# The second exchange of a spectral layer, read back by quarters of the partitions

## The chip, the cores and the metric

The kernel runs on one core of a Trainium2 chip. A core has five engines that run side by side, each through its own list of instructions in order: PE (matrix multiply), DVE and ACT (elementwise work), POOL (more elementwise work) and SP (here it only issues transfers). They share a memory of 128 partitions (SBUF); PE writes into a separate accumulator memory (PSUM) from which DVE and ACT copy. Transfers (DMA) to and from the chip's main memory (DRAM) are issued by SP or ACT and run on 16 transfer engines. An engine waits for another, or for a transfer, at a semaphore. The metric is the device time of one execution in microseconds (us); lower is better.

## The reference

Four layers on a sequence of 2048 rows of 512 values: spectral, attention, spectral, attention, each added to its input.

```python
def _A_ref(x, w_r, w_i):
    B, S, D = x.shape
    X = rfft2(x)                       # over rows and columns
    X = X * (w_r + 1j * w_i)
    return irfft2(X, s=(S, D))
...
x = A_x
x = x + _A_ref(_layernorm(x), A_w_r, A_w_i)
x = x + _B_ref(_layernorm(x), B_wq, B_wk, B_wv, B_wo)
x = x + _A_ref(_layernorm(x), A_w_r, A_w_i)
x = x + _B_ref(_layernorm(x), B_wq, B_wk, B_wv, B_wo)
```

`_A_ref` is the spectral layer, `_B_ref` an attention of 32 heads with one shared key and value. S is 2048 and D is 512.

## The kernel before

Row n of the sequence is 16 p + t: partition p (0 to 127) of tile t (0 to 15). The spectral layer does both transforms as matrix multiplies. The 256 frequencies over the columns are worked on in two halves, h = 0 and 1, of 128 frequencies, real and imaginary part side by side (256 values). The transform over the 2048 rows is split as 128 x 16: `first` sums over p within each tile; then partitions and tiles must change places (the first exchange, through the DRAM tensor D1, with `cross1`); `filtered(j)` sums over the 16 tiles and multiplies by the weights; `back(j)` begins the inverse, 16 points wide; then partitions and tiles change places again (the second exchange, through D2); `along(q, h)` sums over the 128 remaining points with the table CS, two tiles at a time; `last` transforms the columns back and adds x.

The second exchange is what the change is about. Step j of `filtered` and `back` stands for half h = j // 4 and for four of sixteen values of b, 4 (j % 4) to 4 (j % 4) + 3. `back(j)` makes two banks of two b each on PE (lines 213 to 215), ACT copies them to the tile B1 (line 365; DVE does the very last, line 363), and SP writes each copy to D2 (line 366), 128 KB a time; so a half has eight writes. In B1 a partition is (t, a), a from 0 to 7. For `along` the partition must be m = 16 a + b and the tile t. `cross2(h, g)` (line 369) reads tiles 4g to 4g + 3 of half h for all 128 partitions into B2, 256 KB in runs of 512 bytes. Its source spans every b, so each of the four readings depends on all eight writes of its half.

The order of the work is written out by hand: a spectral layer runs under a manual schedule for PE, ACT, DVE and SP, so each engine's instructions stand in the order of the program text. The string STEPS gives the order of `filtered` (f), `back` (b), `joined` (j, the last products of a filter step) and the readings of half 0 (x):

```python
STEPS = "f0 f1 f2 b0 f3 b1 b2 j3 b3 x0 f4 f5 f6 b4 f7 b5 j7 b6 b7"
```

Behind it PE does `along` for half 0, tiles 0 to 15 (line 391, copied to the tile AT by ACT, line 394, and DVE, line 396, in turn). Then come the four readings of half 1: g = 0 and 2 issued by SP, g = 1 and 3 by ACT, behind ACT's four copies. SP goes on with the attention's weights wq and wo (lines 1215 and 1216, in the first spectral layer only). PE does `last` for half 0 of tiles 0 to 3 (lines 404 to 406), then `along` for half 1, one pair of tiles at a time with `last` for both halves of the pair before. The sum goes to x (ACT, line 425), DVE takes the statistics for the next layer norm (line 156), and the keys, values and queries of the attention follow.

In `along`, the contraction is over the 128 partitions of B2, that is over m, against the rows of CS:

```python
nc.tensor.matmul(ps[:, i, :], lhsT=B2[:, h, 2 * q + i, 128 * j:128 * j + 128], rhs=CS[:, j, :], ...
```

The framework tracks which bytes each transfer and instruction reads and writes and puts in the waits; the engine that issues a transfer waits for what the transfer depends on, and everything behind it in that engine's list waits too.

Of the kernel before, what the change touches and what calls it, by code (L numbers as in the profile page):

```python
# [11 lines left out]
P = 128  # L12
BF = mybir.dt.bfloat16
# [32 lines left out]
VCELLS = 128  # L46
LASTW = 6
NEGATE = 7
STEPS = "f0 f1 f2 b0 f3 b1 b2 j3 b3 x0 f4 f5 f6 b4 f7 b5 j7 b6 b7"
NORMED, NORMG = (1,), ((3,), (3,), (3,))  # L50
OUTK, LATE_AT = 2, 4
TWICE = ((7,), 8)
# [23 lines left out]
def host_tables():  # L76
    import ml_dtypes
    bf = lambda a: np.ascontiguousarray(np.asarray(a, dtype=np.float32).astype(ml_dtypes.bfloat16))
    tabs = {}
    p = np.arange(P, dtype=np.float64)  # L80
    m = np.arange(P, dtype=np.float64)
    t16 = np.arange(16, dtype=np.float64)

    row = (128 * np.arange(4)[None, :, None] + np.arange(P)[:, None, None]).astype(np.float64)
    ff = (np.arange(256)[None, None, :] + 1).astype(np.float64)

    half = 2 * np.pi * np.arange(256) / 512.0
    cos, sin = np.cos(half), np.sin(half)
    cos[128], sin[0] = 0.0, 0.0
    cos[129:], sin[129:] = -cos[1:128][::-1], sin[1:128][::-1]  # L90
    turn = (row * ff).astype(np.int64) % 512
    c, s = np.concatenate([cos, -cos])[turn], -np.concatenate([sin, -sin])[turn]
    tabs["PH"] = bf(np.concatenate([c[..., :128], s[..., :128], c[..., 128:], s[..., 128:]], axis=2))

    ang = 2 * np.pi * (16 * p[:, None, None] + t16[None, :, None]) * m[None, None, :] / 2048.0
    tabs["C1"], tabs["S1"] = bf(np.cos(ang)), bf(np.sin(ang))

    ti, ai = np.divmod(np.arange(P), 8)
    same = (ai[:, None] == ai[None, :]).astype(np.float64)
    ang = 2 * np.pi * ti[:, None] * ti[None, :] / 16.0  # L100
    tabs["G"] = bf(np.stack([same * np.cos(ang), same * np.sin(ang), -same * np.sin(ang)], axis=1))

    b16 = np.arange(16, dtype=np.float64)
    mm = 16 * ai[:, None, None] + b16[None, :, None]
    ang = 2 * np.pi * (ti[:, None, None] * t16[None, None, :] / 16.0 + t16[None, None, :] * mm / 2048.0)
    tabs["HC"] = bf(np.stack([np.cos(ang), np.sin(ang), -np.sin(ang)], axis=1))
    tabs["mask8"] = bf(ai[:, None] == np.arange(8)[None, :])

    ang = 2 * np.pi * m[:, None] * p[None, :] / 128.0
    tabs["CS"] = bf(np.stack([np.concatenate([np.cos(ang), np.sin(ang)], axis=1),  # L110
                              np.concatenate([-np.sin(ang), np.cos(ang)], axis=1)], axis=1))

    frow = (128 * np.arange(2)[None, :, None] + np.arange(P)[:, None, None] + 1).astype(np.float64)
    dd = np.arange(512)[None, None, :].astype(np.float64)
    ang = 2 * np.pi * frow * dd / 512.0
    cf = np.where(frow == 256, 1.0, 2.0) / (S * D)
    tabs["PSC"] = bf(cf * np.cos(ang))
    tabs["PSS"] = bf(-cf * np.sin(ang))
    tabs["ident"] = bf(np.eye(P, dtype=np.float32))
    tabs["hmask"] = (np.arange(P)[:, None] // DH % 2 == np.arange(2)[None, :]).astype(np.float32)  # L120
    return tabs


class Tables:


    def __init__(self, nc):
        self.nc, self.host, self.dram = nc, host_tables(), {}
# [82 lines left out]
def rotate(nc, ps, c, s, sn, re_im, first):  # L211

    nc.tensor.matmul(ps, lhsT=c, rhs=re_im, start=True, stop=False, skip_group_check=True)  # L213
    nc.tensor.matmul(ps[:, 0:128], lhsT=s, rhs=re_im[:, 128:256], start=False, stop=False, skip_group_check=True)
    nc.tensor.matmul(ps[:, 128:256], lhsT=sn, rhs=re_im[:, 0:128], start=False, stop=True, skip_group_check=True)  # L215


def spectral_layer(nc, tc, tabs, ht, A_w_r, A_w_i, x_sb, bigp, pre, norm, att, feed, weights):
    C1, S1, S1N, PH, ident = (tabs[n] for n in ("C1", "S1", "S1N", "PH", "ident"))
    with tc.tile_pool(name="workA", bufs=2) as work, tc.tile_pool(name="tabA", bufs=1) as tabA, \  # L220
# [30 lines left out]
            weights(k)  # L251

        D1 = dram.tile([2, 16, P, 256], BF, name="D1")
        D2 = dram.tile([2, P, 16, 256], BF, name="D2")
        turned = len(feed.xT)
        xT = feed.xT[0] if turned else bigp.tile([P, NC, 16, P], BF, name="xT", tag="big")
        Pk, A1, A2 = big("Pk"), big("A1"), big("A2")
# [67 lines left out]
        Z, B1, B2 = big("Z"), big("B1"), big("B2")  # L325
        M = big("M").rearrange("p h t c -> p (h t c)").rearrange("p (i j b r f) -> p i j b r f", i=2, j=4, b=4, r=2)

        def filtered(j):

            h, b4 = j // 4, 4 * (j % 4)  # L330
            hf = slice(128 * h, 128 * h + 128)
            X = work.tile([P, 4, 2, 128], BF, name="X", tag="X", bufs=3)
            for b in range(b4, b4 + 4, 2):
                ps = bank()
                for i in range(2):
                    rotate(nc, ps[:, i, :], G[:, 0, :], G[:, 1, :], G[:, 2, :], A2[:, h, b + i, :], i == 0)
                nc.scalar.copy(out=X[:, b - b4:b - b4 + 2, :, :], in_=ps.rearrange("p j (r f) -> p j r f", r=2))
            m1, m2 = (M[:, i, j % 4] for i in range(2))
            wrb = wr_sb[:, b4:b4 + 4, hf].unsqueeze(2).to_broadcast([P, 4, 2, 128])
            wib = wi_sb[:, b4:b4 + 4, hf].unsqueeze(2).to_broadcast([P, 4, 2, 128])  # L340
            nc.vector.tensor_tensor(out=m1, in0=X, in1=wrb, op=ALU.mult)
            joined()
            nc.vector.tensor_tensor(out=m2, in0=X, in1=wib, op=ALU.mult)
            products.append((j, m1, m2))
# [3 lines left out]
        def joined():  # L348

            while products:  # L350
                j, m1, m2 = products.pop()
                Zv = Z[:, j // 4, 4 * (j % 4):4 * (j % 4) + 4, :].rearrange("p b (r f) -> p b r f", r=2)
                nc.vector.tensor_tensor(out=Zv[:, :, 0, :], in0=m1[:, :, 0, :], in1=m2[:, :, 1, :], op=ALU.subtract)
                nc.vector.tensor_tensor(out=Zv[:, :, 1, :], in0=m1[:, :, 1, :], in1=m2[:, :, 0, :], op=ALU.add)  # L354

        def back(j):
            h, b4 = j // 4, 4 * (j % 4)
            for b in range(b4, b4 + 4, 2):
                ps = bank()
                for i in range(2):  # L360
                    rotate(nc, ps[:, i, :], H1[:, b + i, :], H2N[:, b + i, :], H2[:, b + i, :], Z[:, h, b + i, :], i == 0)
                if j == 7 and b > b4:
                    nc.vector.tensor_copy(out=B1[:, h, b:b + 2, :], in_=ps)
                else:
                    nc.scalar.copy(out=B1[:, h, b:b + 2, :], in_=ps)
                nc.sync.dma_start(out=D2[h, :, b:b + 2, :], in_=B1[:, h, b:b + 2, :])

        def cross2(h, g, eng):
            eng.dma_start(out=B2[:, h, 4 * g:4 * g + 4, :],
                          in_=D2[h].rearrange("(t a) b c -> t (a b) c", t=16)[4 * g:4 * g + 4].rearrange("t m c -> m t c"))  # L370

        for step in STEPS.split():
            j = int(step[1])
            if step[0] == "f":
                filtered(j)
            elif step[0] == "b":
                back(j)
            elif step[0] == "j":
                joined()
            else:  # L380
                for g in range(4):
                    cross2(0, g, nc.sync)

        AT = big("AT").rearrange("p h t c -> p (h t c)").rearrange("p (t h c) -> p t h c", t=16, h=2)

        def along(q, h, use_scalar):

            ps = bank()
            for i in range(2):
                for j in range(2):  # L390
                    nc.tensor.matmul(ps[:, i, :], lhsT=B2[:, h, 2 * q + i, 128 * j:128 * j + 128], rhs=CS[:, j, :],  # L391
                                     start=(j == 0), stop=(j == 1), skip_group_check=True)
            if use_scalar:
                nc.scalar.copy(out=AT[:, 2 * q:2 * q + 2, h, :], in_=ps)
            else:
                nc.vector.tensor_copy(out=AT[:, 2 * q:2 * q + 2, h, :], in_=ps)
# [10 lines left out]

        for q in range(8):
            along(q, 0, q % 2 == 0)
        for g in range(4):  # L410
            cross2(1, g, (nc.sync, nc.scalar)[g % 2])
        weights(20)
        early = 4
        for t in range(early):
# [2 lines left out]
        for q in range(9):  # L417
# [9 lines left out]
            g, odd = divmod(q - 3, 2)  # L427
# [746 lines left out]
def full_kernel(ctx, tc, A_x, A_w_r, A_w_i, B_x, B_wq, B_wk, B_wv, B_wo, out):  # L1174
# [63 lines left out]
    for layer in range(2):  # L1238
        norm_in, norm_out = make_norm(), make_norm()
        spectral_layer(nc, tc, tabs, ht, A_w_r, A_w_i, x_sb, bigp, norm, norm_in, att, feed,  # L1240
                       weights if layer == 0 else lambda k: None)
        feed = attention_layer(nc, tc, att, norm_in, norm_out, x_sb, wo_sb, None if layer == 0 else store)
        norm = norm_out
# [47 lines left out]
```

## Time and profile before

| | us |
|---|---|
| median of 3 runs | 1403.82 (1402.8 to 1404.65) |
| the profiled execution, its time | 1403.77 |
| the profiled execution, its span | 1402.0 |
| PE busy | 1352.2 (96%) |
| ACT busy | 1331.0 (95%) |
| DVE busy | 1309.9 (93%) |
| POOL busy | 844.2 (60%) |

The span runs from the first instruction to the last; the time of an execution has something around it. Busy times are sums over the whole span, most of which is attention. The two spectral layers take roughly the first 90 us and the stretch from about 700 to 785 us. In these the engines are less full, and the transfer engines carry most of what they move in the whole program: 32.62 MB in all.

In lines of the timeline the first two numbers are the start and the duration; then come engine, line, operation, output and inputs, and the number of instructions merged. "SPq" and "ACTq" are the issuing of transfers by SP and ACT, "PEld" the loading of weights into PE. In square brackets stands how long the engine was idle before, and what ended that. "To landing" is the time from the issue of a transfer to its completion.

### The profile page before, as it was taken

Reading aid. Unit: us, or ns where it says so; the run is one execution under the profiler, and the core shown is the slowest. Engines: PE = TensorE matmul, PEld = TensorE weight load, DVE = VectorE, ACT = ScalarE, POOL = GpSimd, SP = SyncE. Lnnn points to the kernel's source line nnn. Section 1 sums busy time; section 2 is a strip of 40 time slices with the busy share of each in tenths; the row PEclk is TensorE's granted clock in tenths of the full one; section 3 lists DMA queues with packets and bytes.
Section 4 is the critical chain, followed back from the end, with each engine's and each line's share of the span. In section 5 each row is a group of like instructions: output and inputs, shape, how many; then the busy total and the mean of one; then the engine's idle time right before and its main releaser. Section 6 shows DMA issues by size and latency. Waiting matters only on the chain.

```text
span 1402.0 us, 34913 instructions
## 1 busy us (share of the span) xinstructions
PE 1352.2 (96%) x14118; PEld 471.5 (34%) x14118; DVE 1309.9 (93%) x2269; ACT 1331.0 (95%) x1542; POOL 844.2 (60%) x503
## 2 busy tenths in 40 slices
PE   7899999999999999999998999999999999999998
PEld 6652232222222222222276422232222222222222
DVE  5689999999999999999966899999999999999997
ACT  6679999999999999999966899999999999999997
POOL 3225666667666667666640267666667667666664
PEclk9999999999999999999999999999999999999999
DMA  8700000000000000001064000000000000000000
GB/s 237 205 24 2 1 2 2 2 1 2 2 2 1 2 2 2 1 1 37 12 173 129 1 2 2 2 2 9 5 6 2 6 9 5 1 5 6 9 2 16
DMA packets 45394, 32.62 MB, mean 23 GB/s; under 512 B 10160, under 2 KB 43312, under 8 KB 44720
## 3 DMA queue, kind: packets, MB, share of 16 engines
q1 hardware_dynamic: 42832, 29.18, 7.3%
q8 instruction: 110, 1.80, 0.5%
q10 hardware_dynamic: 2400, 1.21, 0.3%
q14 instruction: 52, 0.43, 0.1%
HBM read 18.32 MB, written 10.49 MB: 21 GB/s over the span
## 4 chain that ended last, share of the span: by engine, by line
ACT 46%; PE 38%; issue 8%; DVE 6%; DMA 1%; POOL 0%; SPq 0%; DVEq 0%; ACTq 0%
ACT e L1089 45%; PE pv L878 14%; PE sc L923 12%; DVE ph L963 2%; PE aux L923 2%; PE ps L273 2%; PE aux L462 1%; DVE ln_stats L156 1%; PE ps L213 1%; PE aux L691 1%; PE pv L893 1%; DMA B<-D 1%; DVE ph L995 1%; PE ps L391 1%; DMA x_sb<-in_A_x_dram 1%
## 5 line engine op out<-in xcount | busy, mean ns | idle before, releaser
L1089 ACT ACTIVATE e<-sc 128x1024 bf16<-128x1024 f32 x1328 | 1218.1, 1164 | 2.9 <-PE sc L923 2.9
L987 POOL TENSOR_TENSOR ph<-ph,step 128x1024 int32<-128x1024 int32 x404 | 762.8, 1891 | 413.0 <-DVE ph L995 295.8
L963 DVE TENSOR_SCALAR ph<-aux 128x512 uint16<-128x512 f32 x1440 | 905.8, 682 | 20.4 <-PE aux L923 16.2
L878 PE MATMUL pv<-ph,vaug 128*32 128x512 bf16 x4320 | 548.7, 386 | 0.7 <-POOL ph L987 0.3
L923 PE MATMUL sc<-QT,Kv 32*128 32x512 bf16 x2656 | 522.0, 380 | 19.4 <-ACT e L1089 13.9
L878 PE MATMUL pv<-e,vaug 128*32 128x512 bf16 x2656 | 484.0, 384 | 0.3 <-ACT e L1089 0.3
L923 PE MATMUL aux<-QT,Kv 32*128 32x512 bf16 x1440 | 455.9, 384 | 0.0
L923 PEld LDWEIGHTS <-Kv 32*128 32x128 bf16 x4096 | 183.2, 91 | 526.0 <-issue 517.7
L893 PE MATMUL pv<-wo_sb,zeros 128*32 128x512 bf16 x1200 | 257.8, 383 | 0.0
L878 PEld LDWEIGHTS <-vaug 128*32 128x32 bf16 x6976 | 147.6, 94 | 292.6 <-issue 281.6
L995 DVE TENSOR_SCALAR ph<-ph 128x2048 uint16<-128x2048 uint16 x316 | 217.6, 689 | 0.5
L162 POOL TENSOR_TENSOR ln_rstd<-ln_veps,mhalf 128x4 f32<-128x4 f32 x16 | 16.5, 1032 | 109.8 <-DVE ln_veps L161 109.7
L156 DVE BATCH_NORM_STATS2 ln_stats<-x_sb 128x6 f32<-128x512 bf16 x64 | 43.5, 680 | 20.1 <-ACT x_sb L425 14.0
L893 PEld LDWEIGHTS <-zeros 128*32 128x32 bf16 x1200 | 60.1, 94 | 1.9 <-issue 0.3
L793 DVE STREAM_TRANSPOSE oT<-pv 128x512 f32<-128x512 f32 x64 | 45.6, 713 | 9.2 <-PE pv L878 9.2
L185 ACT ACTIVATE Pk<-ps,ln_rstd 128x256 bf16<-128x256 f32 x64 | 26.8, 473 | 19.7 <-PE ps L273 15.2
L462 PE MATMUL aux<-xTa,wq_sb 128*128 128x512 bf16 x120 | 39.5, 385 | 0.4 <-DVE ph L963 0.2
L273 PE MATMUL ps<-tab_PH,xT 128*128 128x256 bf16 x256 | 35.3, 286 | 1.1 <-DVE oT L793 0.8
L287 DVE CAST A<-ps 128x512 bf16<-128x512 f32 x28 | 19.2, 689 | 18.2 <-PE ps L215 17.1
L691 PE MATMUL aux<-wo_sb,ph 128*128 128x512 bf16 x96 | 31.8, 384 | 1.5 <-DVE ph L963 1.0
L815 POOL TENSOR_TENSOR on<-oT,rden 128x512 bf16<-128x512 f32 x30 | 31.7, 1056 | 2.0 <-DVE rden L819 1.8
L213 PE MATMUL ps<-Z,tab_H 128*128 128x256 bf16 x64 | 15.8, 283 | 13.2 <-DVE Z L354 13.2
(109 smaller groups left out, 697.7 us busy)
## 6 DMA issues: line engine op xcount, KB each, us to landing
D<-A SPq DMA_DIRECT2D x32, 128.0 KB, 2.7
A<-D SPq DMA_DIRECT2D x16, 256.0 KB, 3.4
D<-B SPq DMA_DIRECT2D x32, 128.0 KB, 2.9
B<-D SPq DMA_DIRECT2D x12, 256.0 KB, 3.7
wr_sb<-in_A_w_r_dram SPq DMA_DIRECT2D x2, 1024.0 KB, 6.1
wi_sb<-in_A_w_i_dram SPq DMA_DIRECT2D x2, 1024.0 KB, 8.2
out_dram<-x_sb SPq DMA_DIRECT2D x15, 128.0 KB, 1.7
x_sb<-in_A_x_dram SPq DMA_DIRECT2D x3, 512.0 KB, 8.2
```

Of the source, the lines that this page charges most:

```text
L156: nc.vector.bn_stats(st, src)
L273: nc.tensor.matmul(ps[:, j, :], lhsT=xT[:, cc, 2 * k + j, :], rhs=PH[:, cc, 256 * h:256 * h + 256], start=(cc == 0), stop=(cc == NC - 1), ...
L462: self.nc.tensor.matmul(ps, lhsT=w(c), rhs=self.xTq[:, c, qc * 512:(qc + 1) * 512], start=(c == 0), stop=(c == NC - 1), skip_group_check=True)
L691: nc.tensor.matmul(ps, lhsT=OTs[qb][:, g4, kk * P:(kk + 1) * P], rhs=wo_sb[:, g4, :], start=first, stop=last, skip_group_check=True)
L793: end = clock.now(clock.FLIP, lambda: nc.vector.transpose(out=oT[:, par].rearrange("p b c -> p (b c)"), in_=pv), clock.last + clock.MM_END)
L878: nc.tensor.matmul(pv_tiles[gi][32 * i:32 * i + 32, :], lhsT=vaug[:, kc, j, :], rhs=es, start=((gi, i) not in started), stop=(left[gi, i] ...
L893: nc.tensor.matmul(pv_tiles[gi][32 * i:32 * i + 32, :], lhsT=att.zeros, rhs=wo_sb[:, 0, :], start=False, stop=False, skip_group_check=True)
L923: nc.tensor.matmul(out, lhsT=Kv[r, par, kc * P:(kc + 1) * P], rhs=QT[r, g, qb * 512:(qb + 1) * 512], start=True, stop=True, skip_group_che ...
L963: end = clock.now(clock.Z, lambda: nc.vector.tensor_scalar(out=z.bitcast(U16), in0=ps, scalar1=SCALE * LOG2E * 128.0, scalar2=127.0 * 128. ...
L987: nc.gpsimd.tensor_tensor(out=copy.bitcast(I32), in0=z.bitcast(I32), in1=step.to_broadcast([P, w // 2]), op=ALU.add)
L995: nc.vector.tensor_scalar(out=one.bitcast(U16), in0=z.bitcast(U16), scalar1=float(PHASE[1]), scalar2=None, op0=ALU.add)
L1089: nc.scalar.activation(out=e[:, 0:ng * 512], in_=sc[:, 0:ng, :].rearrange("p a b -> p (a b)"), func=ACT.Exp, scale=SCALE)
```

## The change

The readings of the second exchange become quarters of the partitions in place of quarters of the tiles. Quarter g of half h holds the four b that step j = 4 h + g wrote, for all a, and all 16 tiles; so it depends on two writes. D2 gets the shape [2, 4, 128, 4, 256], a block for each step; a write still moves 1 KB for each partition. A reading still moves 256 KB in runs of 512 bytes, now into 32 partitions with 16 tiles each. Partition 32 g + 4 a + b' of B2 then holds m = 16 a + 4 g + b', and the rows of the table CS, made on the host, are put in the same order.

The eight readings are steps of STEPS, all issued by SP: x0 to x3 (half 0) stand together behind b3, where the four readings stood; x4 stands behind b6, and x5, x6 and x7 behind b7. None is left behind `along` of half 0, and none on ACT.

```diff
-STEPS = "f0 f1 f2 b0 f3 b1 b2 j3 b3 x0 f4 f5 f6 b4 f7 b5 j7 b6 b7"
+STEPS = "f0 f1 f2 b0 f3 b1 b2 j3 b3 x0 x1 x2 x3 f4 f5 f6 b4 f7 b5 j7 b6 x4 b7 x5 x6 x7"
...
-                              np.concatenate([-np.sin(ang), np.cos(ang)], axis=1)], axis=1))
+                              np.concatenate([-np.sin(ang), np.cos(ang)], axis=1)], axis=1)[16 * (np.arange(P) // 4 % 8) + 4 * (np.arange(P) // 32) + np.arange(P) % 4])
...
-        D2 = dram.tile([2, P, 16, 256], BF, name="D2")
+        D2 = dram.tile([2, 4, P, 4, 256], BF, name="D2")
...
-                nc.sync.dma_start(out=D2[h, :, b:b + 2, :], in_=B1[:, h, b:b + 2, :])
-
-        def cross2(h, g, eng):
-            eng.dma_start(out=B2[:, h, 4 * g:4 * g + 4, :],
-                          in_=D2[h].rearrange("(t a) b c -> t (a b) c", t=16)[4 * g:4 * g + 4].rearrange("t m c -> m t c"))
+                nc.sync.dma_start(out=D2[h, j % 4, :, b - b4:b - b4 + 2, :], in_=B1[:, h, b:b + 2, :])
+
+        def cross2(h, g):
+            nc.sync.dma_start(out=B2[32 * g:32 * g + 32, h, :, :],
+                              in_=D2[h, g].rearrange("(t a) b c -> t (a b) c", t=16).rearrange("t m c -> m t c"))
...
-                for g in range(4):
-                    cross2(0, g, nc.sync)
+                cross2(j // 4, j % 4)
...
-        for g in range(4):
-            cross2(1, g, (nc.sync, nc.scalar)[g % 2])
```

Behind line 369 the line numbers of the changed kernel are one to three lower: 391 becomes 390, 394 becomes 393, 1089 becomes 1086.

## The prediction

> **What bounds the kernel now.** I read the page first. Over the whole span ACT (95%), PE (96%) and DVE (93%) are nearly full, and ACT's exponentials on line 1089 hold 45% of the chain that ended last. The diff touches none of that. It touches the end of the two spectral layers (about 40 to 76 us and 735 to 770 us), so I went to those stretches: the chain of waits, then the timeline, then the landings of single transfers. The page's table of transfers has the kinds that matter:
>
> ```profile
> D<-B SPq DMA_DIRECT2D x32, 128.0 KB, 2.9
> A<-D SPq DMA_DIRECT2D x16, 256.0 KB, 3.4
> B<-D SPq DMA_DIRECT2D x12, 256.0 KB, 3.7
> B<-D ACTq DMA_DIRECT2D x4, 256.0 KB, 3.9
> ```
>
> D<-B is a write of `back` into D2, B<-D a reading of the second exchange, A<-D a reading of the first exchange (256 KB into 32 partitions, in runs of 8 KB). The timeline of the first layer, where frequency half 1 is handed over (start, duration, engine, line):
>
> ```profile
> 60.43 2.58 SPq L366 DMA_DIRECT2D D<-B  x4
> 61.46 3.66 PE L391 MATMUL ps<-tab_CS,B 128*128 128x256 bf16 x32
> 64.71 0.92 SPq L369 DMA_DIRECT2D B<-D  x2
> 65.00 0.99 ACTq L369 DMA_DIRECT2D B<-D  x2
> 67.32 0.38 PE L406 MATMUL ps<-tab_PSS,AT 128*128 128x512 bf16 x1
> 67.45 0.85 PEld L391 LDWEIGHTS <-B 128*128 128x128 bf16 x8 [0.24 <-DMA B<-D]
> 68.18 1.07 ACT L394 CAST AT<-ps 128x512 bf16<-128x512 f32 x2 [2.88 <-DMA B<-D]
> ```
>
> The last write is issued at 62.6 and lands 2.0 later, at 64.6; that frees SP to issue the first reading at 64.71, which lands 2.7 later at 67.41. Meanwhile PE does half 0 (line 391) and four tiles of `last`, and is out of work at 67.3. So the whole wait for the exchange on PE is 0.24 us, and all after it (PE is busy without a gap until past 76 us) starts from there. The second layer has the same place with no wait at all:
>
> ```profile
> 753.27 2.26 SPq L366 DMA_DIRECT2D D<-B  x4
> 757.34 0.92 SPq L369 DMA_DIRECT2D B<-D  x2
> 760.16 0.97 PEld L391 LDWEIGHTS <-B 128*128 128x128 bf16 x8
> ```
>
> Its first reading lands at 757.34 + 2.7 = 760.04, just ahead of 760.16. The later readings (tiles 4 to 15) land behind their need nowhere: line 391 waits for a transfer once in the trace, those 0.24 us. **So there is 0.24 us to win, and PE has no slack in which to hide a later landing.**
>
> **The change, part by part.**
>
> *Half 0 (x0 to x3).* Same place in SP's order, but each waits for two writes instead of eight, so three of the four can go out from 52.1, when SP has issued b3's writes, instead of 53.9; the last still waits until 53.9. `along` on half 0 starts at 61.4, when PE comes to it, and the old readings had landed by 59.8. Worth 0. Were the cover gone (1.6 us of it), each us beyond would be on the path.
>
> *ACT's two issues (0.99 us at 65.00)* go to SP. ACT sits idle there for 2.88 us, so this is 0. SP's wq and wo loads move behind the fourth reading; wq lands at 72.7 and is first used at 81.2, so a few us late costs 0.
>
> *CS permuted:* same table, same size, same matmuls: 0.
>
> *What `along` on half 1 needs.* Before, its first two pairs of tiles need one reading of four (4 tiles in all 128 partitions). After, every matmul contracts over all partitions, so the first one needs **all four quarters**, the last of which may be asked for only when b7's second write has landed. Three things decide when that is.
>
> (1) x4 stands on SP between b6's writes and b7's. Queued behind it: b7's two writes, x5 to x7, wq, wo. Its own wait is for b4's writes, long landed. Its issue takes 0.37 to 0.50 (the readings' row on SP). In layer 2 SP is free at 754.15 and b7's first cast ends at 754.64, so the issue is hidden. In layer 1 the second of b6's writes took 1.12 to issue (60.9 to 62.05) where 0.32 is usual; without that stretch x4 goes at 61.3, with it at 62.1, and b7's writes go 0.4 later too.
>
> (2) x4's 256 KB stand in the transfer queue ahead of b7's writes. That they are served in order is seen at half 0 of layer 2: readings issued at 747.5, 748.0, 748.5, 749.1 land after 2.9, 3.3, 4.2, 4.5 (at 750.4, 751.3, 752.7, 753.6), and the writes issued from 749.6 on, which alone take 1.9 to 2.0, land only behind them, at 754.8, 755.2, 755.6, 755.9. So a queued reading costs (753.6 - 750.4)/3 = 1.07, in layer 1 (59.8 - 56.6)/3 = 1.07 too, and a queued write 0.4.
>
> (3) The cost of a reading into 32 partitions in runs of 512 B has no row. Its neighbours:
>
> ```profile
> L369 SPq DMA_DIRECT2D B<-D x1: 370/370/370, 757.3 to 757.3; - x1
> DMA to landing us min/median/max: 2.7/2.7/2.7
> ...
> L291 SPq DMA_DIRECT2D A<-D x1: 409/409/409, 733.7 to 733.7; - x1
> DMA to landing us min/median/max: 3.1/3.1/3.1
> ```
>
> 512 B runs over 128 partitions: 2.7. 8 KB runs into 32 partitions: 3.1 (others 3.1 to 3.4). The first shares the length of run, the second the partitions, so I bound the new one by both: lone landing 2.7 to 3.1, queued 1.07 to 1.07 + 0.4 = 1.47. I take the middle, 2.9 and 1.27, since it shares one trait with each. No reason favours less than 1.07: the bytes and the runs are the same.
>
> [...]
>
> *Layer 2, by landings.* x4: 754.15 + 2.9 = 757.05. b7's writes: 757.45, 757.85 (before: 757.2). x5, x6, x7 follow in the queue: 759.1, 760.4, 761.65. (From its issue alone x7 would land at 757.9 + 2.9 = 760.8, so the queue decides.) PE was ready at 760.16: **1.5 us late.**
>
> *Layer 1.* x4 at 61.3: lands 64.2, writes 64.6 and 65.0 (before 64.6), x7 68.8, against a start at 67.45: 1.35. With SP's stretch, x4 at 62.1: x7 69.6, 2.15. One of the two layers shows the stretch at this place; I take the middle, **1.75**.
>
> What is late next is all of PE's work to the end of the layer, then the keys and queries, then the exponentials: PE has no gap after this point in which to catch up, so the delay passes on whole. **Sum: 1.5 + 1.75 = 3.25 us.** The profiled execution took 1403.77 (span 1402.0 and 1.77 around it), the median of the runs shown is 1403.82: 1403.8 + 3.2 = **1407.0 us**. Low bound (2.7 and 1.07, no stretch): layer 2 x7 at 760.86, 0.7; layer 1 at 68.0, 0.55; 1405.0. High bound (3.1 and 1.47, with the stretch): 762.5 and 70.4, so 2.3 + 3.0 = 5.3; 1409.1.
>
> **The rivals.** A: quarters cost what whole readings cost. The low bound, 1405.0. For it: 512 runs of 512 B either way. Against it: A<-D's 3.1 to 3.4.
>
> B, not slower: x4 to x6 don't delay b7's writes, because they are spread over time and the queue is empty when the writes come; then the last write lands at 64.6 and 757.2 as before, x7 alone decides, and with 2.7 it lands at 67.4 and 760.0, when PE asks for it. 1403.8 at no gain; the most there is to win is the 0.24 us wait, 1403.6. It decides from the point where x4 drains before b7's writes start to move. For it: the queue is idle between 757 and 758 us. Against it: x4 is issued at most 0.6 us ahead of b7's first write, and the served order of (2).
>
> C, much slower: a queued quarter costs 1.6 or more and a lone one 3.4 (the slowest undisturbed A<-D). Then x7 lands at 763.15 and 70.3: 3.0 and 2.85 late. An idle PE of that length has a price of its own, seen once in this trace:
>
> ```profile
> 40.90:44.90 4.00, 1.47 (x21) 1.26 (x20) 4.00 (x8) 1.64 (x5) 0.14 (x1) 0.99 0.66 201
> 44.90:48.30 3.40, 2.94 (x22) 2.33 (x21) 2.62 (x7) 2.64 (x5) 0.00 (x0) 0.51 0.99 244
> 58.00:61.40 3.40, 1.90 (x23) 1.64 (x24) 2.47 (x6) 1.95 (x5) 0.00 (x0) 1.00 0.73 230
> ```
>
> (Window, length, busy PE, PEld, DVE, ACT, POOL, granted clock, share of the transfer engines, GB/s.) PE idled from 40.9 to 43.6, and the clock was 0.51 in the 3.4 us after; the idling around 58 us (1.5 us of 3.4) brought nothing. Half speed for 3.4 us of unbroken PE work is 1.7 us, in both layers 3.4: 1403.8 + 5.85 + 3.4 = 1413.0. [...]
>
> That the change doesn't do what it says I can exclude: the built order of SP's instructions has the readings where the diff puts them, with waits for two writes each.
>
> **How the numbers follow.** Forecast 0.52, A 0.2, B 0.13, C 0.15. What a measurement of this kernel can tell from no change is about 0.2%, 2.8 us, so "slower" begins at 1406.6. The forecast lies at that edge: some 0.66 of its chance is above it (0.34), C all of it (0.15), A almost none (0.01): slower 0.50. Faster by over 2.8 us would need something to win of which the profile shows 0.24 us: 0.03. Same 0.47. The range reaches from B's end, 1403.6, past the high bound of 1409.1 to 1410.2, and leaves out most of C. The forecast's own range is 1405.0 to 1409.1.
>
> **What would show it.** Right: line 390 (391 before) waits 1 to 2 us for B<-D once in each layer, then goes on with no further wait; b7's second write lands 0.4 to 0.7 later than before; readings of a quarter lie further apart than 1.07. Wrong: no wait there, or a wait of 0.24 as now (B); a granted clock below 1.0 around 70 us (C); a wait on `along` of half 0 at 61 us, which I put at nothing; or a difference that lies in the attention stretches, which I hold to be untouched.

## The result, and the profile after

| | before | after |
|---|---|---|
| median of 4 runs, us | 1403.62 (1402.8 to 1404.65) | 1412.19 (1410.4 to 1413.23) |
| profiled execution: time, span | 1403.77, 1402.0 | 1411.36, 1409.6 |
| granted clock, mean | 0.999 | 0.997 |

The changed kernel is slower: ratio 1.0058, 95% interval 1.0045 to 1.007, some 8.6 us. The forecast was 1407.0, and its range ended at 1410.2.

The two profiled executions can be laid side by side, because the programs differ in nothing but the exchange. I took four places in each: PE's first matmul of `along` on half 0, its first on half 1, the first exponential of the attention, and the end.

| stretch | before, us | after, us | difference |
|---|---|---|---|
| start to half 0, layer 1 | 61.46 | 61.79 | +0.33 |
| half 0 to half 1, layer 1 | 6.08 | 9.38 | +3.30 |
| half 1 to the first exponential | 26.06 | 27.18 | +1.12 |
| first exponential to half 0, layer 2 | 660.69 | 660.96 | +0.27 |
| half 0 to half 1, layer 2 | 6.09 | 8.67 | +2.58 |
| half 1 to the first exponential | 26.05 | 26.05 | 0.00 |
| first exponential to the end | 615.53 | 615.54 | +0.01 |

So 5.9 of the 7.6 us lie in the two hand-overs of half 1 and 1.1 in one stretch behind the first. The other 0.6 lie ahead of a hand-over, and other kernels show them too: the start to half 0 took 60.4 to 62.4 us in the runs below, and the stretch of 660.96 is also that of `tiles_sp`, which costs nothing. The timeline of the first hand-over after the change:

```profile
61.67 0.93 SPq L369 DMA_DIRECT2D B<-D  x1
61.79 3.66 PE L390 MATMUL ps<-tab_CS,B 128*128 128x256 bf16 x32
62.69 0.91 SPq L366 DMA_DIRECT2D D<-B  x2
63.70 2.62 SPq L369 DMA_DIRECT2D B<-D  x3
71.14 0.99 PEld L390 LDWEIGHTS <-B 128*128 128x128 bf16 x6 [3.60 <-issue]
71.17 1.22 PE L390 MATMUL ps<-tab_CS,B 128*128 128x256 bf16 x5 [3.13 <-DMA B<-D]
```

SP issues x4, b7's two writes, x5 to x7; PE has half 0 behind it as before, and now stands idle for 3.13 us where it stood for 0.24. In the second layer:

```profile
759.31 3.66 PE L390 MATMUL ps<-tab_CS,B 128*128 128x256 bf16 x32
767.95 0.78 PEld L390 LDWEIGHTS <-B 128*128 128x128 bf16 x8 [2.89 <-issue]
767.98 1.03 PE L390 MATMUL ps<-tab_CS,B 128*128 128x256 bf16 x8 [2.42 <-DMA B<-D]
```

The chain of waits through this place (start, duration, what) names the two links:

```profile
760.46 2.92 DMA D<-B
763.45 4.39 DMA B<-D
767.98 0.61 PE ps L390 x4
```

b7's second write takes 2.9 us to land instead of 2.0, and the last quarter, asked for when it has landed, takes 4.4 instead of the 2.7 of the first reading by tiles. From the write's landing to the landing that PE needs it was 2.83 and 2.84 us before, and is 5.08 and 4.45 now.

The clock, in windows (length; busy PE, PEld, DVE, ACT, POOL; granted clock; share of the transfer engines; GB/s):

```profile
67.50:70.90 3.40, 0.54 (x3) 0.04 (x1) 0.00 (x0) 0.00 (x0) 0.00 (x0) 1.00 1.08 228
70.90:74.30 3.40, 3.13 (x12) 1.60 (x13) 0.00 (x0) 1.54 (x3) 0.00 (x0) 0.50 0.50 160
764.90:768.30 3.40, 0.98 (x7) 0.42 (x5) 0.00 (x0) 0.00 (x0) 0.00 (x0) 1.00 0.47 70
768.30:771.70 3.40, 3.16 (x22) 1.83 (x20) 1.16 (x3) 2.88 (x6) 0.00 (x0) 1.00 0.00 0
```

Behind the wait of layer 1 the clock is 0.50 for 3.4 us; behind that of layer 2 it stays at 1.00 in this execution. The four executions are ordered by their mean clock: 1410.4 at 0.999, 1411.36 at 0.997, 1413.02 and 1413.23 at 0.995. The profiled one is the second, 0.8 us below the median.

### The profile page after: what moved, and what is told of

It reads as the page before. It is cut to its first block, busy times and chain, and to the rows that moved or that the text cites. A ratio compares the mean times of both kernels' runs of the same rounds, so it can differ in the third digit from the quotient of the medians.

```text
span 1409.6 us, 34846 instructions
## 1 busy us (share of the span) xinstructions
PE 1342.2 (95%) x14050; PEld 470.7 (33%) x14118; DVE 1310.9 (93%) x2269; ACT 1331.2 (94%) x1542; POOL 845.1 (60%) x503
## 4 chain that ended last, share of the span: by engine, by line
ACT 50%; PE 31%; issue 9%; DVE 7%; DMA 3%; POOL 0%; SPq 0%; DVEq 0%; ACTq 0%
ACT e L1086 48%; PE pv L875 12%; PE sc L920 10%; DVE ph L960 3%; PE aux L920 2%; PE ps L273 1%; DVE ln_stats L156 1%; PE ps L213 1%; DVE ph L992 1%; PE aux L459 1%; DMA D<-A 1%; DMA B<-D 1%; PE aux L688 1%; PE pv L890 1%; DVE M L341 1%
## 5 line engine op out<-in xcount | busy, mean ns | idle before, releaser
L459 PE MATMUL aux<-xTa,wq_sb 128*128 128x512 bf16 x90 | 32.6, 384 | 2.8 <-issue 2.4
L688 PE MATMUL aux<-wo_sb,ph 128*128 128x512 bf16 x72 | 26.1, 383 | 3.6 <-issue 2.1
```

What stands on the lines that cost most here:

```text
L459: self.nc.tensor.matmul(ps, lhsT=w(c), rhs=self.xTq[:, c, qc * 512:(qc + 1) * 512], start=(c == 0), stop=(c == NC - 1), skip_group_check=True)
L688: nc.tensor.matmul(ps, lhsT=OTs[qb][:, g4, kk * P:(kk + 1) * P], rhs=wo_sb[:, g4, :], start=first, stop=last, skip_group_check=True)
```

## The experiments

Each kernel's ratio is taken to runs of the kernel before on the same chip, whose median was 1404.5 for half1_tiles, reversed, strided and x4last, 1404.48 for half0_tiles, early_spread, early6 and warm, and 1405.1 for tiles_sp and warm11. "Interval" is the stretch from half 0 to half 1, in the two layers; the wait is that of PE's matmuls in front of half 1, or of its weight load where it is 0.5 or less. The kernels after, early6, warm and warm11 exchange the data in the same way, and their intervals still differ by 1.3 us in layer 1 (9.38 to 10.72) and by 0.5 in layer 2 (8.46 to 8.99); smaller differences between single traces say little.

| kernel | median, us | ratio (95%) | interval, us | PE's wait, us |
|---|---|---|---|---|
| before | | 1 | 6.08, 6.09 | 0.24, 0 |
| after | 1412.19 | 1.0058 (1.0045 to 1.007) | 9.38, 8.67 | 3.13, 2.42 |
| half1_tiles | 1404.53 | 0.9999 (0.999 to 1.0008) | 6.29, 6.26 | 0.5, 0.5 |
| half0_tiles | 1413.39 | 1.0059 (1.0045 to 1.0073) | 9.86, 8.19 | 3.61, 1.94 |
| reversed | 1412.46 | 1.0059 (1.0044 to 1.0074) | 9.17, 8.89 | 2.91, 2.65 |
| tiles_sp | 1404.79 | 1.0 (0.9991 to 1.0009) | 6.27, 6.08 | 0.5, 0 |
| strided | 1409.18 | 1.0036 (1.0024 to 1.0048) | 8.44, 7.67 | 2.20, 1.42 |
| x4last | 1413.0 | 1.0055 (1.0038 to 1.0072) | 9.81, 8.82 | 3.57, 2.57 |
| early_spread | 1407.43 | 1.0023 (1.0013 to 1.0032) | 7.89, 7.40 | 1.65, 1.15 |
| early6 | 1411.01 | 1.0046 (1.003 to 1.0061) | 10.41, 8.50 | 2.87, 0.96 |
| warm | 1411.33 | 1.0047 (1.0034 to 1.0059) | 9.52, 8.99 | 1.77, 1.22 |
| warm11 | 1410.97 | 1.0038 (1.0025 to 1.0052) | 10.72, 8.46 | 2.10, 0 |

**half1_tiles: half 1 undone alone**, its readings by tiles (`cross2t`) from a tensor in the old layout.

```diff
-STEPS = "... b3 x0 x1 x2 x3 f4 f5 f6 b4 f7 b5 j7 b6 x4 b7 x5 x6 x7"
+STEPS = "... b3 x0 x1 x2 x3 f4 f5 f6 b4 f7 b5 j7 b6 b7"
...
+        for g in range(4):
+            cross2t(1, g, (nc.sync, nc.scalar)[g % 2])
```

> The changed kernel with half 1 undone: its readings by tiles into 128 partitions, behind all eight writes, two on SP and two on ACT as in the kernel before; half 0 by quarters as in the changed kernel. CS holds both orders of rows (256 KB loaded instead of 128). If all of the loss is half 1's: 1403 to 1405. If the slower queue of half 0's quarters delays b4's to b7's writes and so half 1: b7's second write lands 0.5 us or more later and the time is 1405 or above.

The time is that of the kernel before, though each interval is 0.2 us longer. b7's second write lands 0.07 and 0.25 us later than before, counted from the start of half 0, and not the 0.5 of the second guess. The loss is half 1's, and half 0's quarters with their permuted rows cost next to nothing.

**half0_tiles: half 0 undone alone**, the mirror image (half 0 by tiles behind all eight writes, half 1 by quarters).

> The changed kernel with half 0 undone: its four readings by tiles into 128 partitions, behind all eight writes; half 1 by quarters as in the changed kernel. If the loss is all half 1's own: 1410 to 1413, waits of 2.4 to 3.1 as in the changed kernel. If half 0's slow quarters add to it through the queue: 1 us or more below the changed kernel.

The time is the changed kernel's. The wait moves between the layers (3.61 and 1.94), but the two intervals add up to 18.05 us, as in the changed kernel. With intervals that differ between traces as said above, so close an agreement may be chance.

**reversed: the kernel before, the last reading needed first.**

```diff
-        for g in range(4):
-            cross2(1, g, (nc.sync, nc.scalar)[g % 2])
+        for g in (3, 2, 1, 0):
+            cross2(1, g, nc.sync)
```

> The kernel before, with the four readings of half 1 (4 tiles in 128 partitions each) all on SP and in the order g = 3, 2, 1, 0, so that the first work on half 1 needs the reading that was issued last. It measures by itself what it costs to need all four. If needing all four is a cost of its own: the reading of tiles 0 to 3 lands at 2.7 + 3 x 1.07 = 5.9 after the first issue, PE waits about 3.2 us in each layer, 1410 to 1412. If four readings in a row are nearly as quick as one: under 1 us a layer, 1404 to 1405.

**tiles_sp: its control**, the same with `range(4)`.

> The kernel before with the four readings of half 1 all on SP in the order g = 0, 1, 2, 3: the control for the reversed order, from which it differs in that order alone. If in the reversed order it was needing the last reading that cost: no wait of more than 0.3 us before half 1, 1403.5 to 1405. If it was SP issuing all four: 1410 or above as there.

The two kernels differ only in which of four equal transfers goes out first. Their second layer:

```profile
761.49 2.02 SPq L369 DMA_DIRECT2D B<-D  x4
767.43 0.77 PEld L391 LDWEIGHTS <-B 128*128 128x128 bf16 x8 [3.14 <-DMA B<-D]
767.43 1.05 PE L391 MATMUL ps<-tab_CS,B 128*128 128x256 bf16 x8 [2.65 <-DMA B<-D]
```

```profile
757.82 2.02 SPq L369 DMA_DIRECT2D B<-D  x4
760.70 0.97 PEld L391 LDWEIGHTS <-B 128*128 128x128 bf16 x8
760.91 1.04 PE L391 MATMUL ps<-tab_CS,B 128*128 128x256 bf16 x8
```

In the first, `reversed`, PE starts 5.9 us after the first issue, in the second, `tiles_sp`, 2.9, with no wait. With the old transfers untouched, needing the last of four instead of the first costs as much as the whole change. That the two totals are equal is in part chance: `reversed` asks for all four behind the last write, the changed kernel asks for three of them earlier and pays more for each. The wait of 0.5 in the control's first layer is 0.2 more than I allowed, and its time is that of the kernel before: SP can issue all four without loss.

**strided: the quarters spread over the partitions.**

```diff
-            nc.sync.dma_start(out=B2[32 * g:32 * g + 32, h, :, :],
+            nc.sync.dma_start(out=B2[g::4, h, :, :],
```

(and the rows of CS to match)

> The changed kernel, with quarter g of the partitions spread: partitions g, g+4, g+8 ... instead of 32 g to 32 g + 31 (CS permuted to match). Same bytes, same runs of 512 B, same waits, same order. Theory (few partitions side by side make a reading slow): a lone quarter lands in 2.7 to 2.9 instead of 3.3, queued ones lie 1.1 apart instead of 1.35, PE's wait before half 1 falls from 3.1 and 2.4 us to about 0.5 to 1.0, the clock stays at 1.0, time about 1405 to 1406. Rival (it is only that all four readings are needed, whatever they cost): waits and time as in the changed kernel, about 1412.

The time came between the two guesses. The part on price was half right. At half 0 four quarters stand in the queue in a row. The changed kernel, then this one, in windows over that place in layer 2:

```profile
752.00:756.00 4.00, 2.93 (x36) 2.52 (x36) 3.68 (x9) 2.65 (x7) 0.00 (x0) 1.00 1.24 186
```

```profile
750.00:754.00 4.00, 2.35 (x31) 2.04 (x30) 4.00 (x9) 2.65 (x7) 0.00 (x0) 1.00 0.92 265
```

(The last two numbers are the share of the transfer engines and GB/s.) Side by side the engines are busy all the time and move 186 GB/s, spread they move 265 with time to spare. By landings, quarters side by side are 1.35 and 1.37 us apart, spread ones 0.97 and 0.93, less than the 1.07 of the old readings. A lone quarter, however, did not get cheaper:

```profile
L369 SPq DMA_DIRECT2D B<-D x1: 387/387/387, 749.7 to 749.7; - x1
DMA to landing us min/median/max: 3.3/3.3/3.3
```

```profile
L369 SPq DMA_DIRECT2D B<-D x1: 607/607/607, 748.6 to 748.6; - x1
DMA to landing us min/median/max: 3.3/3.3/3.3
```

3.3 us for the first of half 0 in both, against 2.7 to 2.9 by tiles. The intervals are 0.94 and 1.00 us shorter than in the changed kernel. So about 1 us a layer of the loss is the partitions lying side by side, and the waits of 2.20 and 1.42 that stay are not. The clock was halved once, behind the first wait (0.78 on average from 68.0 to 71.4, 0.71 from 71.4 to 74.8).

**x4last: x4 out of the way of b7's writes.**

```diff
-STEPS = "... b6 x4 b7 x5 x6 x7"
+STEPS = "... b6 b7 x4 x5 x6 x7"
```

> The changed kernel with x4 moved from before b7's writes to behind them. Rival theory (x4's place in the queue ahead of b7's writes is what costs): b7's second write lands about 1 us sooner and the fourth quarter with it, time 1409 to 1410. My theory (the four slow quarters in a row are the cost): the write lands sooner, but the four now queue behind it, 3.3 + 3 x 1.37 after the first's issue, so the last lands within 0.4 us of where it did, time 1411 to 1413.

In layer 2 the last write lands 1.9 after its issue, and the last quarter 5.9 behind that (in the changed kernel 2.9 and 4.45). What the write gains, the readings lose. The rival falls; the queue holds the same work in another order. In this trace the clock is halved behind both waits, twice in a row behind the first (0.65 on average from 68.0 to 71.4, 0.50 from 71.4 to 74.8), and from half 1 to the first exponential it is 28.37 and 27.32 us; so its time of 1413.09 holds some 3.6 us of clock.

**early_spread: both remedies**, the spread quarters and x4 ahead of b6.

```diff
-STEPS = "... b5 j7 b6 x4 b7 x5 x6 x7"
+STEPS = "... b5 x4 j7 b6 b7 x5 x6 x7"
```

> The spread quarters (partitions g, g+4, ...) with x4 moved ahead of b6, so that it has drained before b7's writes, and x5, x6, x7 behind b7. Theory (what is left of the loss is x4's delay of b7's writes, 0.9 us, and the last quarter's own 3.3 us): b7's second write lands 2.0 after its issue, the last quarter 3.3 after that, or up to 0.5 later if x5 and x6 still drain; PE's wait 0.5 to 1.0 in each layer, 1404.8 to 1406.5, clock at 1.0. Rival (three quarters in the queue behind the write hold it up as four do, as they did side by side): wait 1.4 to 2.2 as with the spread quarters alone, 1408 to 1410.

Neither number came out: 1407.43, between the two. x4 now delays b6's writes and these b7's (in layer 2 the second lands 2.5 after its issue), and the last quarter takes its 3.3 (3.6 in layer 1). In the profiled execution, 1406.37, the clock is not halved behind the wait of layer 1 (1.00 from 68.0 to 74.8). It is the best form of the change that I ran, and still slower than the kernel before.

**early6: more work in the wait.**

```diff
-        early = 4
+        early = 6
```

> The changed kernel with six tiles of last's first half ahead of half 1 instead of four: 6 matmuls, 1.3 us of PE work, move into the wait in each layer. If the delay is PE's wait alone and passes on whole: 1.3 us less in each layer and the idle stretch too short for the half clock, 1407.5 to 1409.5. If the accumulator banks run out (six sums and two pairs are all eight): the work waits elsewhere and the time stays at 1411 or above.

A miss, and a telling one. In layer 2 the wait shrinks to 0.96, yet from the first matmul on half 1 to the first exponential it is 25.93 us instead of 26.05: 1.3 us of PE's work taken out of that stretch win 0.1. The chain of waits in that stretch goes by other engines (this kernel's own lines):

```profile
768.28 0.61 PE ps L390 x4
768.92 0.59 ACT AT L393
770.20 0.59 ACT x_sb L422
770.82 0.70 DVE ln_stats L156
771.73 0.59 DVE ln_stats L156
772.52 0.59 DVE ln_stats L156
```

ACT's copy of each new sum and DVE's statistics on it set the pace. In layer 1 the clock was halved all the same (0.74 on average from 71.4 to 74.8; the stretch is 27.25).

**warm and warm11: idle matmuls in the wait**, seven and eleven.

```diff
+        ps = psum.tile([P, 512], F32, name="ps", tag="pa")
+        for _ in range(7):
+            nc.tensor.matmul(ps, lhsT=ident, rhs=PSC[:, 0, :], start=True, stop=True, skip_group_check=True)
         for q in range(9):
             if q < 8:
                 along(q, 1, True)
```

> The changed kernel with seven idle matmuls (128x512, about 0.215 us each, 1.5 us in all, result unused) on PE behind the four early tiles, inside the wait for half 1. They end before the last quarter lands, so half 1 starts when it did. Theory (PE's idle stretch of 2.4 to 3.1 us halves its clock for 3.4 us, and that is part of the loss): no window of half clock after the wait in either layer, time 1409.5 to 1410.5 and less spread between executions (the changed kernel: 1410.4 to 1413.2). Rival (the half clock costs nothing, the path goes over other engines): 1412 with the same spread.

> The changed kernel with eleven idle matmuls (2.4 us) on PE in the wait for half 1, where seven left an idle stretch of 1.8 and 1.2 us and one window of half clock. They end before the last quarter lands in both layers. Theory (half clock is a part of the loss): idle stretch under 1 us, no window of half clock after either wait, executions close together at 1409.5 to 1410.5. Rival (half clock costs nothing): 1411 to 1413 as before.

With seven the idle stretch of layer 1 was still 1.77 us, and the clock was halved behind it in the profiled execution:

```profile
68.70:72.10 3.40, 1.39 (x11) 0.82 (x10) 0.00 (x0) 0.77 (x2) 0.00 (x0) 1.00 1.09 285
72.10:75.50 3.40, 3.40 (x11) 1.52 (x10) 1.70 (x4) 2.06 (x5) 0.00 (x0) 0.50 0.06 20
```

The median, 1411.33, is above the 1409.5 to 1410.5 expected. With eleven, though its last quarter landed late and PE still idled 2.10, no halved window followed:

```profile
70.90:74.30 3.40, 1.64 (x11) 1.02 (x12) 0.00 (x0) 1.07 (x2) 0.00 (x0) 1.00 0.62 199
74.30:77.70 3.40, 3.40 (x22) 1.94 (x20) 2.63 (x7) 3.14 (x7) 0.00 (x0) 1.00 0.00 1
```

and from half 1 to the first exponential it is 26.06 us, as in the kernel before, against 27.18 in the changed kernel. So a halved window cost 1.1 us there. It is not a fixed price: the same stretch with one halved window is 27.06 in reversed, 27.57 in half0_tiles and 27.74 in warm, 1.0 to 1.7 us above 26.06. The executions of warm11 lie between 1409.4 and 1411.3 instead of 1410.4 and 1413.2; its median, 1410.97, is still above what I expected, and the intervals of the two ratios overlap, so the medians alone wouldn't show it. The stretches do.

## Why the prediction was wrong

The direction and the place were right: a wait for B<-D once a layer in front of half 1, none anywhere else, nothing in the attention. The size failed, in two places. The wait for the exchange was put at 3.25 us, and the profiled execution shows 5.88 in the same two intervals. And the forecast left out the halved clock behind the wait, which stood in rival C alone; it cost 1.12 us in that execution. Without the clock the time would have been about 1403.8 + 5.9 = 1409.7, below the 1410.2 at which its range ended.

- *No slack on PE for a later landing, 0.24 us to win:* no run contradicts it. half1_tiles and tiles_sp, with waits of up to 0.5 us, are level with the kernel before; reversed, whose wait is 2.7 to 2.9, is not.
- *Half 0, ACT's issues, CS: 0.* Right, by half1_tiles, half0_tiles and tiles_sp.
- *The first work needs all four quarters:* right, and the root of it. reversed shows that this alone, at the old price of a reading, costs all of the 0.6%. I had it in the text; its size then hung on the sum over the queue.
- *(1) x4's issue in front of b7's writes:* 0.24 and 0.23 us later than before, relative to the start of half 0. I had 0.4 in layer 1 if SP's stretch came again, and nothing in layer 2. In layer 1 the stretch came at x4's own issue, which took 0.93.
- *(2) b7's second write lands 0.4 to 0.65 later:* undersized. It was 1.04 and 1.15. The write lands 0.74 and 0.81 behind x4, as forecast (0.8), but x4 itself landed 0.7 and 0.5 later than I had it (in layer 1 without the stretch).
- *(3) and the sum, x5, x6 and x7 in the queue at 1.27 each:* **this is the step that failed.** From the landing of b7's second write to that of the last quarter I had 3 x 1.27 = 3.8 us. It was 2.01 + 1.38 + 1.69 = 5.08 and 2.26 + 1.37 + 0.82 = 4.45. That is 1.9 of the 2.6 us that the sum lacks, and the first quarter behind the write alone makes 1.7 of it; x4's later landing makes the rest. A queued quarter in the row at half 0 took 1.35 to 1.37, inside my bounds, so the price of a queued quarter was only a little low; the sum took no account of the first reading behind a write being dearer than the next ones. The spread quarters show the same: 1.60 and 1.73 behind the write, against 0.93 to 0.97 in a row. Why, no run shows.
- *A lone quarter at 2.9, at most 3.1:* the first quarter of half 0 took 3.3 to 3.4, and x4 itself 3.54 (its slow issue included) and 3.01. The upper bound of 3.1 was near the fastest of the sixteen A<-D readings; the median in the prediction's own table is 3.4. With 3.35 and 1.36 in its sum the prediction would have had 4.7 us, about 1408.5: the two prices alone don't explain the miss.
- *wq and wo behind the fourth reading: 0.* Not shown to be 0. In layer 1 wq is issued 0.36 us behind x7, its packets of 1 KB run beside x7's from 68.0 us on, and x7 lands 1.69 behind x6; in layer 2, without these loads, 0.82. No run leaves the loads out, so their share is open.
- *The queue decides, not x7's own issue:* right for the changed kernel. With spread quarters x7 lands 3.3 after its own issue in layer 2, so there both bounds meet.
- *The delay passes on whole:* right in the table (26.05 both times in layer 2), but for the wrong reason. It is not that PE is without a gap; early6 shows that ACT and DVE pace that stretch in layer 2.
- *Rival C:* nearest, though I gave it 0.15. It had waits of 2.85 and 3.0 (3.13 and 2.42 came) and the halved clock behind them. That its time came so near is in part luck: its queued quarter of 1.6 was not measured (1.35 to 1.37), and it had a halved window in both layers, where the profiled execution has one. It priced a window at 1.7, half of 3.4; 1.12 was measured here, and 1.0 to 1.7 in the other traces. That in some executions the clock is halved in both layers, which would lift the median above the profiled 1411.36, fits the order of the runs by clock. No trace of the changed kernel shows it, but that of x4last does: 1413.09 us at a mean clock of 0.995, as in the two slowest executions of the changed kernel.
- *Rivals A and B* fell: quarters cost more than whole readings, and b7's writes were delayed.

A queued quarter at half 0 took 1.35 with its partitions side by side and 0.95 with partitions g, g+4, ... (strided), while the lone 3.3 is the same in both. Why side by side costs more in the queue, no run shows. Why a lone quarter at half 0 takes 0.4 to 0.7 us more than a reading by tiles there (2.7 to 2.9) stays open; no run here separates the number of partitions from the 16 pieces in each.

## What to carry to other kernels

Ask of a split transfer not only what each part waits for, but how many parts the consumer's first instruction needs. Cutting along the consumer's loop (by tiles) let PE start after one of four; cutting along the contraction made it need all four, the last bound to the last write, and the earlier readings then compete with that write in the queue: in layer 2 it took 2.9 us to land instead of 2.0. If the destination must be a subset of the partitions, spread it with a step over all of them; here that was worth 1 us a layer.

## What the runs showed of the hardware

- With readings of 256 KB in runs of 512 B in a row, the transfers moved 186 GB/s into 32 neighbouring partitions (after) and 265 into every fourth partition (strided).
- An idle PE of 1.77 us was followed by a halved clock for 3.4 us (warm), one of 2.10 us was not (warm11), nor 2.42 us in layer 2 of the changed kernel: in these traces the length of the gap alone does not decide. Nor does PE's busy time in any 3.40 us: it was 1.39 just ahead of the halved window of warm, and 0.98 from 764.90 to 768.30 in the changed kernel, behind which the clock stayed at 1.00. So the prediction's reading, that an idle stretch near 3 us does it and 1.5 us does not, is not borne out: 1.77 us was enough here, and 2.42 us was not. What decides is not shown here.
